# Chunks of 512 tokens, and one TensorE step for the scores of one head pair and the v products of another

## The chip, the cores and the metric

The kernel runs on one core of a Trainium2 chip. The metric is the device time of one execution in microseconds (us). Before the change it was 943.15 us, the median of three runs (941.31 to 943.30).

## The reference

```python
def _attn_ref(q, k, v):                      # [8, 8, 576, 64], fp32
    q_d, k_d, v_d = mean of 4 neighbouring positions of q, k, v      # 144 positions
    out_d = sm_attn(q_d, k_d, v_d)           # softmax(q k^T / 8) v
    out_up = np.repeat(out_d, 4, axis=2)
    mask = np.abs(pos[:, None] - pos[None, :]) < 4                   # a band of 7
    scores = np.where(mask, scale * np.matmul(q, k.transpose(0, 1, 3, 2)), -1e9)
    ... softmax with sum + 1e-9 ...
    return out_up + np.matmul(attn, v)

x = attn_out.transpose(0, 2, 1, 3).reshape(4608, 512)
h = x @ w_in                                 # [4608, 2048]
g = h * np.clip(h + 3.0, 0.0, 6.0) / 6.0
return g @ w_out                             # [4608, 512]
```

(The lines are shortened.) There are two attentions per head, one over pooled positions ("pooled") and one in a band of seven ("banded"); their sum goes through one gated expert layer.

## The kernel before, in words

**The expert layer** is nearly all of TensorE's time. Its tokens go through in chunks (`PART`): 512, 256, then ten of 384. In a chunk there are 16 blocks f of 128 hidden columns. The first product of a block (`gemm1`, L934) is 12 matmuls as wide as the chunk: four pieces of 128 model columns, each as high x high, high x low and low x high, since x and the weights are split into a rounded part and a rest (fp32r). It writes one of two banks, h0 and h1. ScalarE takes relu from it (L940), VectorE the gate (L944), which frees the bank; ScalarE makes the rounded part (L948) and VectorE or GpSimd the rest (L952). The second product (`gemm2`, L986) takes three matmuls of 512 columns for each 128 tokens of the chunk, adds up over the 16 blocks in the o banks (one for each 128 tokens), and follows two blocks behind. ScalarE or VectorE take the o banks out (L882, L884). Each chunk's x is split just ahead of it (`plan_split`, lines 120, 122 and 837), after the last first product of the chunk before.

**The attention** runs in units: one of 8 batches and one of four pairs of heads. Units of batches 0 and 1 ("alone") are worked with TensorE transposes in the start and during the first chunk. From batch 2 on a unit does this: q and k are loaded and turned by VectorE in blocks of 32 (L318), summed over four positions (L327, L331 and L333); TensorE makes the pooled scores (`scores_d4`, L442, 6 matmuls with two records each) and the banded ones (`scores`, L615, 20 matmuls with two records each) in three `a` banks; the pooled softmax is done by ScalarE with sums given out by the exp itself (`weigh`, L463); the banded one adds a mask (L629), takes the greatest (L470), subtracts (L473), one exp over 640 columns (L476), sums (L479), and multiplies by the reciprocal (L492). Both go to memory and come back turned (`put`, `get`, `turn_l`, `turn_d`; L555, L536). Later the v products (`pv`, L656, and `pv_d4`, L570) go into two `a` banks, and the mean (L594, L597) and the additions (L664) write x. The v rows are summed over four by L376 on VectorE or L378 and L379 on GpSimd.

**The order.** A planner (`Plan.emit`) orders all operations before the kernel is built, by a table of costs and due times; each engine then runs its list in that order. Operations name the buffers that they take and free, and the planner gives a slot (`_slots`) when one is free. `plan_duo` makes two units; a unit is a generator, and its second part (v products) is made one unit behind. Scores and v products are operations of their own there.

Of the kernel before, what the change touches and what calls it, by code (L numbers as in the profile page):

```python
# [19 lines left out]
P = 128  # L20
# [36 lines left out]
def tile_local_down_attention_moe(ctx, tc, q_all, k_all, v_all, _qk_loc, _v_loc, w_in, w_out, ident_d, _mask_d, out):  # L57
# [177 lines left out]
    def plan_duo(b, d, masked):  # L235
# [50 lines left out]
        for u in range(2):  # L286
            unit = plan_unit(b, d, u, row0, k0, kv, PS, qk, evicts, users, masked, early_user, due - (1 - u) * unit_time(b))
            next(unit)
            units.append(unit)
            if b < ALONE or len(units) > 1:  # L290
                next(units.pop(0), None)
        if b < BY_PE:
            for kind in "qk":
                plan.free_after(("qkd" + k0, (kind, b, d)), users[kind])

    def plan_unit(b, d, u, row0, k0, kv, PS, duo, evicts, users, masked, early_user, due):
# [11 lines left out]
        def ldt(t, kind):  # L308
            st["raw", kind] = raw = buf("raw" + k0, (kind, un), [P, S // 32, 32])
# [6 lines left out]
        def turn(kind):  # L316
            qk[kind] = buf("qk" + k0, (kind, un), [P, S])
            nc.vector.transpose(out=qk[kind], in_=st["raw", kind].rearrange("p j i -> p (j i)"))  # L318
# [16 lines left out]
        for kind, t in (("q", q_all), ("k", k_all)):  # L335
# [3 lines left out]
            else:  # L339
                rk = "raw" + k0, hk  # L340
                l = op("SP", 2.0, partial(ldt, t, kind), loads if b == 1 else [], take=[rk], size=dma(4 * S, 128), nd=4)
                a = turned[kind] = [op("DVE", 0.66, partial(turn, kind), [l], take=[("qk" + k0, hk)], free=[rk])]
# [88 lines left out]
        def scores_d4():  # L431

            st["psd"] = bank(PS, ("sd", un))
            st["pd"] = buf(pk[0], pk[1], [P, 3, SD])
# [3 lines left out]
            for h, j in ((0, 0), (1, 1), (0, 2), (1, 0), (0, 1), (1, 2)):  # L438
                hs = slice(h * D, (h + 1) * D)
                a, n = QPLACE[h][j]  # L440
                ps = st["ps", 1][:, 5 * D:] if n == 1 else st["psd"][:, n // 2 * SD:]
                nc.tensor.matmul(  # L442
                    ps[a * D:(a + 1) * D, :SD], q4[hs, j * QSTEP:j * QSTEP + QS], k4[hs], start=True, stop=True,
                    skip_group_check=True)
# [4 lines left out]
        def rows_d4(i):  # L449

            if i == 0:
                return [st["psd"][:, :2 * SD].rearrange("p (j k) -> p j k", j=2)] + [st[x][:, ::2] for x in ("pd", "md", "sd")]
            return [st["ps", 1][:, 5 * D:5 * D + SD].unsqueeze(1)] + [st[x][:, 1:2] for x in ("pd", "md", "sd")]
# [23 lines left out]

        def total(x, s):
            nc.vector.tensor_reduce(out=s, in_=x, op=ALU.add, axis=AX.X)  # L479

        def plus(s):
            nc.gpsimd.tensor_scalar(s, s, 1e-9, None, op0=ALU.add)
# [49 lines left out]
        def turn_d(i):  # L532
            if "pdt" not in st:
                st["pdt"] = buf(tk_d[0], tk_d[1], [P, 18 * NAR])
            n, a, e = (P, 0, 12 * NAR) if i == 0 else (NAR, 12 * NAR, 18 * NAR)
            nc.vector.transpose(  # L536
                out=st["pdt"][:n, a:e], in_=st["rd"][:n].rearrange("p j k -> p (j k)")[:, a:e])
# [7 lines left out]
        def get():  # L545
            st["rl"] = raw = buf("rl", un, [P, 20, NAR])
# [6 lines left out]
        def turn_l():  # L553
            st["pt"] = buf("PT" + kv, ("l", un), [P, 5, 2 * D])
            nc.vector.transpose(  # L555
                out=st["pt"].rearrange("p j q -> p (j q)"), in_=st["rl"].rearrange("p j k -> p (j k)"))
# [44 lines left out]
        def scores():  # L601

            st["p"] = buf(pl[0], pl[1], [P, 5, 2, D])
            stats = buf("st" + k0, ("l", un), [P, 2, 12])
            st["m"], st["s"] = stats[:, 0, :NWIN], stats[:, 1, :NWIN]
            for g in range(2 if alone else 0):
# [21 lines left out]
        def outside(g):  # L628
            nc.vector.tensor_tensor(  # L629
# [16 lines left out]
        def pv():  # L646
            if not direct:
# [21 lines left out]
        def tail(eng):  # L669

            if "tail" not in early:
                early["tail"] = xt[0, "tail"] = buf(*xb_of(0), [P, NHP, S - TOK0])
            copy_on(eng, xt[0, "tail"][:, hp], st["px"][1][:, TOK0 - HALF:HALF])
# [6 lines left out]
        def scores_all():  # L680
# [836 lines left out]
```

## Time and profile before

| | us |
|---|---|
| median of three runs | 943.15 |
| lowest, highest run | 941.31, 943.30 |
| span of the profiled execution | 940.1 |
| TensorE busy in it | 925.5 |
| VectorE, ScalarE, GpSimd busy | 564.6, 358.8, 306.1 |

The profile is of one execution; its own time is the span and the little that lies around it, 3.0 us up to the median. In the views that follow, PE is TensorE, PEld its weight loads, DVE VectorE, ACT ScalarE, POOL GpSimd and SP the engine that issues DMAs. A row of grouped instructions gives line, engine, operation, output and input with shapes, the count, then busy us and mean ns of one, then the idle time before them and what ended it. A matmul's busy time overlaps its neighbours', so a product's price is read from the chain, where each row is start, length, engine, output, line and records.

### The profile page before, as it was taken

The numbers are of one execution on the slowest core, as the hardware profiler recorded it, in microseconds if no ns is written. First come the engines' busy times: TensorE is split into PE (matmuls) and PEld (weight loads), VectorE is DVE, ScalarE is ACT, GpSimd is POOL, SyncE is SP. The second block draws the span as 40 slices with busy tenths as digits, with TensorE's granted clock in tenths as the row PEclk, the third lists the DMA queues.
The fourth block names the chain that finished last, engine by engine and source line by source line (L and its number), as shares of the span: only waits on it lengthen the run. The fifth ranks groups of instructions, "written<-read, shape, count | busy, mean of one in ns | idle before, by whom it ended". The sixth has DMA issues, their size and how long they took to land.

```text
span 940.1 us, 19730 instructions
## 1 busy us (share of the span) xinstructions
PE 925.5 (98%) x7525; PEld 803.9 (86%) x7525; DVE 564.6 (60%) x1048; ACT 358.8 (38%) x889; POOL 306.1 (33%) x396
## 2 busy tenths in 40 slices
PE   6999999999999999999999999999999999999997
PEld 4577778989889888889889888988988988998996
DVE  7999987487767566554456667445455654323322
ACT  4799654334333233323333333323233432221322
POOL 4654444244452343332334344225125320000000
PEclk9999999999999999999999999999999999999999
DMA  7997154356666555544235555645154430100101
GB/s 210 311 287 221 30 131 97 67 105 129 125 128 125 108 118 111 101 88 107 39 82 119 101 105 103 129 99 101 37 98 88 104 64 6 35 1 3 32 1 33
DMA packets 311758, 93.52 MB, mean 99 GB/s; under 512 B 251376, under 2 KB 297840, under 8 KB 311664
## 3 DMA queue, kind: packets, MB, share of 16 engines
q1 hardware_dynamic: 311376, 91.83, 43.6%
q8 instruction: 59, 0.97, 0.4%
q10 hardware_dynamic: 288, 0.43, 0.2%
q14 instruction: 35, 0.29, 0.1%
HBM read 69.60 MB, written 22.61 MB: 98 GB/s over the span
## 4 chain that ended last, share of the span: by engine, by line
PE 93%; SPq 2%; DMA 2%; DVE 1%; issue 1%; ACT 1%; POOL 0%; DVEq 0%; ACTq 0%
PE h L934 42%; PE o L986 40%; PE a L656 2%; PE a L615 2%; PE a L442 1%; PE a L570 1%; PE a L986 1%; DMA arena<-in_v_dram 1%; SPq L311 1%; PE o L589 1%; PE a L501 0%; PE a L589 0%; SPq L351 0%; PE a L428 0%; DMA arena<-pl 0%
## 5 line engine op out<-in xcount | busy, mean ns | idle before, releaser
L934 PE MATMUL h<-rounded,wp 128*128 128x384 f32 (+2 forms) x2240 | 418.8, 336 | 0.0
L986 PE MATMUL o<-wp,rounded 128*128 128x512 f32 x1680 | 408.3, 394 | 0.0
L934 PEld LDWEIGHTS h<-rounded,wp 128*128 128x128 f32 x2240 | 383.9, 188 | 14.0 <-issue 1.6
L986 PEld LDWEIGHTS o<-wp,rounded 128*128 128x128 f32 x1680 | 311.0, 188 | 65.8 <-issue 4.2
L940 ACT ACTIVATE arena<-h 128x384 f32<-128x384 f32 (+2 forms) x192 | 93.7, 490 | 366.9 <-PE h L934 365.2
L944 DVE SCALAR_TENSOR_TENSOR arena<-arena,h 128x384 f32<-128x384 f32 (+2 forms) x192 | 104.9, 547 | 183.8 <-ACT arena L940 182.8
L948 ACT CAST rounded<-arena 128x384 fp32r<-128x384 f32 (+2 forms) x192 | 98.2, 512 | 120.5 <-DVE arena L944 120.0
L952 DVE TENSOR_TENSOR rounded<-arena,rounded 128x384 fp32r<-128x384 f32 (+2 forms) x140 | 84.9, 606 | 77.1 <-PE o L986 42.2
L952 POOL TENSOR_TENSOR rounded<-arena,rounded 128x384 fp32r<-128x384 f32 (+2 forms) x52 | 54.5, 1048 | 149.0 <-ACT rounded L948 92.9
L331 POOL TENSOR_TENSOR arena<-arena 128x144 f32<-128x144 f32 x35 | 15.7, 449 | 180.1 <-PE a L442 101.1
L318 DVE STREAM_TRANSPOSE arena<-arena 128x576 f32<-128x576 f32 x56 | 43.2, 772 | 23.7 <-PE a L615 9.0
L333 POOL TENSOR_TENSOR arena<-arena 128x144 f32<-128x144 f32 x70 | 45.1, 644 | 5.5
L492 POOL TENSOR_TENSOR arena<-arena 128x640 f32<-128x640 f32 (+1 forms) x31 | 37.7, 1216 | 18.2 <-DVE arena L485 14.6
L837 POOL TENSOR_TENSOR rounded<-arena,rounded 128x384 fp32r<-128x384 f32 (+2 forms) x12 | 16.3, 1372 | 71.2 <-ACT rounded L120 71.0
L473 POOL TENSOR_TENSOR arena<-arena 128x640 f32<-128x640 f32 x21 | 26.5, 1260 | 27.4 <-DVE arena L470 17.2
L463 ACT ACTIVATE arena<-a,arena 128x144 f32<-128x144 f32 x87 | 32.5, 378 | 1.9 <-DMA arena<-in_v_dram 0.2
L376 DVE TENSOR_REDUCE arena<-arena 128x128 f32<-128x512 f32 (+1 forms) x25 | 26.8, 1072 | 7.2 <-PE a L570 7.1
L536 DVE STREAM_TRANSPOSE arena<-arena 128x384 f32<-128x384 f32 (+1 forms) x48 | 21.4, 461 | 15.2 <-DMA arena<-pd 12.9
L615 PE MATMUL a<-arena 64*64 64x64 f32 x1200 | 30.0, 223 | 0.0
L205 POOL TENSOR_TENSOR wp<-early,wp 128x1024 fp32r<-128x1024 f32 (+1 forms) x9 | 19.3, 2148 | 29.0 <-ACT wp L201 16.8
L615 PEld LDWEIGHTS a<-arena 64*64 64x64 f32 x1200 | 25.6, 134 | 2.1 <-issue 2.1
L656 PEld LDWEIGHTS a<-arena 64*64 64x64 f32 x1120 | 19.1, 134 | 9.3 <-issue 8.1
(194 smaller groups left out, 822.7 us busy)
## 6 DMA issues: line engine op xcount, KB each, us to landing
rawp<-in_w_in_dram SPq DMA_DIRECT2D x16, 512.0 KB
rawp<-in_w_out_dram SPq DMA_DIRECT2D x16, 512.0 KB
arena<-in_q_dram SPq DMA_DIRECT2D x112, 72.0 KB
arena<-in_k_dram SPq DMA_DIRECT2D x112, 72.0 KB
pl<-arena SPq DMA_DIRECT2D x24, 320.0 KB
arena<-pl SPq DMA_DIRECT2D x96, 80.0 KB
arena<-in_v_dram SPq DMA_DIRECT2D x28, 256.0 KB
out_dram<-arena SPq DMA_DIRECT2D x91, 72.0 KB
```

What stands on the lines that cost most here:

```text
L318: nc.vector.transpose(out=qk[kind], in_=st["raw", kind].rearrange("p j i -> p (j i)"))
L333: eng.tensor_tensor(t, t, x[:, :, r], op=ALU.add)
L463: nc.scalar.activation(p[:, j], x[:, j], AF.Exp, bias=m[:, j:j + 1], scale=1.0 / 128.0, accum_out=s[:, j:j + 1])
L492: eng.tensor_tensor(x, x, s.unsqueeze(2).broadcast_to(list(x.shape)), op=ALU.mult)
L615: nc.tensor.matmul(st["ps", g][half:half + WIN, jj * D:jj * D + WIN], qk_of("q")[hs, k_first:k_first + WIN], qk_of("k")[hs, k_first:k_firs ...
L656: nc.tensor.matmul(st["px"][g][h * D:(h + 1) * D, at + lo:at + hi], st["v"][ks, jj, h * D:(h + 1) * D], st["pt"][ks, jj, half + lo:half + ...
L934: nc.tensor.matmul(st["ps"], win[f][:, wt, kk * P:(kk + 1) * P], xs[part][:, kk], start=(kk == 0 and i == 0), stop=(kk == NK - 1 and i == ...
L940: nc.scalar.activation(st["t"], st["ps"], AF.Relu, bias=3.0)
L944: nc.vector.scalar_tensor_tensor(out=t, in0=t, scalar=6.0, in1=st["ps"], op0=ALU.min, op1=ALU.mult)
L948: nc.scalar.copy(st["gh"], st["t"])
L952: eng.tensor_tensor(st["gl"], st["t"], st["gh"].bitcast(F32), op=ALU.subtract)
L986: nc.tensor.matmul(otile[n, m], gt[:, ms], wout[f][:, wt], start=(f == 0 and i == 0), stop=(f == NF - 1 and i == 2),)
```

## The change

- All chunks have 512 tokens (nine). The o banks become four, the `a` banks two. The cost tables of the planner keep their scale (`SHARE`).
- From batch 2 on one operation (`plan_burst`, "a shared step") has the pooled scores of a new unit, both v products of the unit two before it (`DEPTH = 2`), and the banded scores of the new one. It takes both h banks: the v products go there, and the third of the pooled scores that does not fit in the `a` banks, as four matmuls of 72 columns (`rest`), which are copied out (`pull`).
- The turns of q, k and of the weights that come back write over their input (`turn`, `turn_d`, `turn_l`); q, k and the pooled weights share five buffers.
- The banded softmax gets its sums from the exp: ten exps of 64 columns with a bias and a sum (`exps_sums`) take the place of the subtraction, one exp and VectorE's sum. The added 1e-9 goes from GpSimd to ScalarE.
- The buffers between the expert products: three for rounded parts (were four) and two for rests (were three). Due times of the attention (`UNIT_T`, `SLACK`) are others.

```diff
-TOK, TOK0 = 384, 512
+TOK, SHARE = 512, 384
-PART = [(0, TOK0), (TOK0, 2 * TOK - TOK0)] + [(t, TOK) for t in range(2 * TOK, B * S, TOK)]
+PART = [(t, TOK) for t in range(0, B * S, TOK)]
...
+    def plan_burst(unit):
+
+        new = next(unit) if unit else None
+        old = next(units[0]) if len(units) == DEPTH or units and not unit else None
...
+        hx = [(f"h{g}x", key) for g in range(2)]
+
+        def burst():
+            hb = [bank(*h) for h in hx]
+            if new:
+                new["pooled"](hb)
+            if old:
+                old["pv"](hb)
+            if new:
+                new["banded"]()
...
+        o = op("PE", cost, burst, [a for x in both for a in x["after"]], take=hx + [t for x in both for t in x["take"]],
+               free=[t for x in both for t in x["free"]], lag=LAGT, rec=52 * len(both))
...
         def turn(kind):
-            qk[kind] = buf("qk" + k0, (kind, un), [P, S])
-            nc.vector.transpose(out=qk[kind], in_=st["raw", kind].rearrange("p j i -> p (j i)"))
+            nc.vector.transpose(out=qk[kind], in_=qk[kind])
...
+                for i in range(2 if n == 2 else 1):
+                    ks = slice(i * SD // 2, (i + 1) * SD // 2) if n == 2 else slice(0, SD)
+                    ps = rest(h, i) if n == 2 else rows_d4(n)[a * D:(a + 1) * D]
+                    nc.tensor.matmul(
+                        ps, q4[hs, j * QSTEP:j * QSTEP + QS], k4[hs, ks], start=True, stop=True, skip_group_check=True)
+
+        def rest(h, i):
+            return st["hb"][h][i * D:(i + 1) * D, HALF + SD:HALF + SD + SD // 2]
...
+        def exps_sums(first, x, m, s):
+
+            for j in range(first, first + 2):
+                nc.scalar.activation(
+                    x[:, j], x[:, j], AF.Exp, bias=m[:, j:j + 1], scale=0.125, accum_out=s[:, j:j + 1])
...
         def plus(s):
-            nc.gpsimd.tensor_scalar(s, s, 1e-9, None, op0=ALU.add)
+            nc.scalar.activation(s, s, AF.Copy, bias=1e-9)
...
-            ("xb", 2, NHP * S * 4), ("t", 2, TOK * 4), ("rl", 1, NWIN * D * 4), ("ob", 1, 2048), ("raw", 4, S * 4), ("qk", 4, S * 4),
+            ("xb", 2, NHP * S * 4), ("t", 2, TOK * 4), ("ob", 1, 2048), ("raw", 2, 4 * ROW * 4), ("qk", 5, S * 4),
...
-    for key, n in (("gh", 4), ("gl", 3)):
+    for key, n in (("gh", 3), ("gl", 2)):
...
-        ... "a": ["a0", "a1", "a2"], "s": ["a0", "a1", "a2", "o0", "o1", "o2"], "h": ["h0", "h1"],
-        "o0": ["o0"], "o1": ["o1"], "o2": ["o2"], "o3": ["a2"]})
+        ... "a": ["a0", "a1"], "s": ["a0", "a1", "o0", "o1", "o2", "o3"], "h": ["h0", "h1"], "h0x": ["h0"], "h1x": ["h1"],
+        "o0": ["o0"], "o1": ["o1"], "o2": ["o2"], "o3": ["o3"]})
```

What the planner makes of it, at three places. The first is TensorE in the middle of the attention, before: two first products, three second ones, a unit's v products (L656 banded, L570 pooled), and on. (The number behind a name tells buffers apart.)

```order
L934 MATMUL h_4250<-rounded,wp_645 128x384 x12
L986 MATMUL o_3560<-wp_1773,rounded 128x512 x3
L986 MATMUL o_3568<-wp_1773,rounded 128x512 x3
L986 MATMUL o_3575<-wp_1773,rounded 128x512 x3
L656 MATMUL a_4292<-arena 64x60 x2
...
L656 MATMUL a_4293<-arena 64x60 x2
L570 MATMUL a_4292<-arena 64x144 x2
L570 MATMUL a_4293<-arena 64x144 x2
```

And in the changed kernel, with a shared step among 12 second products on either side:

```order
L981 MATMUL h_2362<-rounded,wp_1029 128x512 x12
L1031 MATMUL o_2103<-wp_1149,rounded 128x512 x3
...
L1031 MATMUL o_2163<-wp_1149,rounded 128x512 x3
L472 MATMUL a_2418<-arena 64x144 x2
L472 MATMUL a_2419<-arena 64x144 x2
L472 MATMUL h_2416<-arena 64x72 x2
L472 MATMUL h_2417<-arena 64x72 x2
L709 MATMUL h_2416<-arena 64x60 x2
...
L617 MATMUL h_2417<-arena 64x144 x2
L617 MATMUL h_2416<-arena 64x144 x2
L666 MATMUL a_2418<-arena 64x64 x2
...
L1031 MATMUL o_2103<-wp_1289,rounded 128x512 x3
```

The v products have moved between the two kinds of scores of another unit and from the a banks into the h banks, which the first products before (h_2362) and after it use too.

The second place is VectorE behind v products, before: a v sum (L376), the mean's second half (L597), the additions (L664), then the next rest and gates.

```order
L376 TENSOR_REDUCE arena<-arena 128x128
L597 SCALAR_TENSOR_TENSOR arena<-a_4293,arena 128x144
L485 RECIPROCAL arena<-arena 128x10
L664 TENSOR_TENSOR first<-a_4292,arena 128x288
L664 TENSOR_TENSOR first<-a_4293,arena 128x288
L952 TENSOR_TENSOR rounded<-arena,rounded 128x384
L944 SCALAR_TENSOR_TENSOR arena<-arena,h_4356 128x384
```

In the changed kernel, around a shared step: turns of q and k (L346) stand between the last gates ahead of the step, and a v sum (L403) or a sum of k (L355) beside the mean and the additions (L644, L717).

```order
L346 STREAM_TRANSPOSE arena<-arena 128x576
L991 SCALAR_TENSOR_TENSOR arena<-arena,h_3615 128x512
L346 STREAM_TRANSPOSE arena<-arena 128x576
L991 SCALAR_TENSOR_TENSOR arena<-arena,h_3641 128x512
L999 TENSOR_TENSOR rounded<-arena,rounded 128x512 x2
L403 TENSOR_REDUCE arena<-arena 128x128
L644 SCALAR_TENSOR_TENSOR arena<-h_3690,arena 128x144
L355 TENSOR_REDUCE arena<-arena 128x144
L717 TENSOR_TENSOR arena<-h_3689,arena 128x288
L717 TENSOR_TENSOR arena<-h_3690,arena 128x288
L682 TENSOR_TENSOR arena<-a_3691,mask 128x5x64
```

The gate and the additions have become what frees an h bank for a shared step and for the first product after it.

The third place is TensorE where the first chunk ends, before: 24 second products lie ahead of the next chunk's first product (h_1843).

```order
L986 MATMUL a_941<-wp_1670,rounded 128x512 x3
L986 MATMUL o_874<-wp_1773,rounded 128x512 x3
L986 MATMUL o_882<-wp_1773,rounded 128x512 x3
L986 MATMUL o_888<-wp_1773,rounded 128x512 x3
L986 MATMUL a_941<-wp_1773,rounded 128x512 x3
L934 MATMUL h_1843<-rounded,wp_531 128x256 x12
```

In the changed kernel the scores of batch 2's second unit stand directly ahead of it (h_1972), behind 12 second products:

```order
L1031 MATMUL o_920<-wp_1786,rounded 128x512 x3
L472 MATMUL a_1930<-arena 64x144 x2
L472 MATMUL a_1931<-arena 64x144 x2
L472 MATMUL h_1928<-arena 64x72 x2
L472 MATMUL h_1929<-arena 64x72 x2
L666 MATMUL a_1930<-arena 64x64 x2
...
L981 MATMUL h_1972<-rounded,wp_563 128x512 x12
```

The first scores of batch 2 have moved from the second chunk into the end of the first one.

More of the change, by code (lines that the diff above doesn't have):

```diff
@@ L287, in plan_duo @@
             unit = plan_unit(b, d, u, row0, k0, kv, PS, qk, evicts, users, masked, early_user, due - (1 - u) * unit_time(b))
[L288 to L291, printed above, removed]
+            if b < ALONE:
+                for _ in unit:
+                    pass
+            else:
+                plan_burst(unit)
         if b < BY_PE:
@@ L605, in scores @@
             st["m"], st["s"] = stats[:, 0, :NWIN], stats[:, 1, :NWIN]
+        def scores():
+            if alone:
+                places()
             for g in range(2 if alone else 0):
@@ L646, in pv @@
         def pv():
-            if not direct:
+            if alone and not direct:
                 st["px"] = [bank(PS, ("x", un, g)) for g in range(2)]
@@ L1064, in tile_local_down_attention_moe @@
                 break
-        if not duos and units:
-            next(units.pop(0), None)
+        while not duos and units:
+            plan_burst(None)
         plan_split(n, prev_last)
@@ L1201, in start_of @@
 def start_of(n):
-    return T0 + TC * sum(size for _, size in PART[:n]) / TOK
+    return T0 + TC * sum(size for _, size in PART[:n]) / SHARE
 def need_chunk(b):
```

189 lines of the change are left out of this document (96 added, 93 removed).

## The prediction

> **What bounds the kernel now.** I read the page first (busy times, then the chain that ended last), then the table of stretches, then the list of TensorE's waits, and last the chain row by row.
>
> ```profile
> span 940.1 us, 19730 instructions
> PE 925.5 (98%) x7525; PEld 803.9 (86%) x7525; DVE 564.6 (60%) x1048; ACT 358.8 (38%) x889; POOL 306.1 (33%) x396
> PE 93%; SPq 2%; DMA 2%; DVE 1%; issue 1%; ACT 1%; POOL 0%; DVEq 0%; ACTq 0%
> 60.00:80.00 20.00, 20.00 (x142) 15.36 (x141) 20.00 (x28) 18.45 (x25) 13.41 (x8) 1.00 0.81 239
> 200.00:250.00 50.00, 50.00 (x479) 44.12 (x478) 35.15 (x67) 18.73 (x54) 20.31 (x28) 1.00 0.60 121
> 800.00:900.00 100.00, 100.00 (x510) 91.45 (x509) 31.70 (x54) 25.74 (x51) 1.95 (x1) 1.00 0.06 17
> PE o L638 <- ACT early L120: 0.4, 1, 0.4
> PE a L656 <- ACT arena L463: 0.2, 1, 0.2
> ```
>
> In the stretches the columns are TensorE, its weight loads, VectorE, ScalarE, GpSimd, the granted clock and DMA. TensorE is full in each, at clock 1.00, in the attention stage (200:250) as in the pure matmul stage (800:900). Its waits after the start are fractions of a microsecond. So the time is the start, a sum of TensorE work, and a short end; the other engines count only where they make TensorE wait. Next, TensorE's pieces in the chain (start, length, line, records), from three places:
>
> ```profile
> 130.51 2.72 PE h L934 x12
> 137.86 2.73 PE h L934 x12
> 144.91 2.76 PE h L934 x12
> 177.96 2.87 PE h L934 x24
> 240.86 4.19 PE h L934 x24
> 245.05 0.51 PE a L442 x9
> 245.56 0.06 PE a L615 x2
> 245.62 0.07 PE a L442 x2
> 245.69 0.58 PE a L615 x32
> 246.27 4.35 PE o L986 x18
> 250.62 4.19 PE h L934 x24
> 254.81 0.74 PE a L656 x40
> 255.54 0.48 PE a L570 x12
> 256.03 4.30 PE o L986 x18
> 265.94 4.12 PE o L986 x18
> ```
>
> L934 is the first expert product with 512 (130 to 147), 256 (178) and 384 tokens (241); L986 is the second; L442 and L615 are one head pair's scores, L656 and L570 its v products. One product costs 2.737/12 = 0.2281 us at 512, 2.87/24 = 0.1196 at 256, 4.19/24 = 0.1746 at 384; the second product 4.12/18 = 0.2289.
>
> **The change, part by part.**
>
> *Chunks of 512.* Before: 192 first products at 512, 192 at 256, 10 x 192 at 384: 43.8 + 23.0 + 335.2 = 402.0 us. After: 9 x 192 = 1728 at 512: 394.2. That is -7.8. Ends: with the second product's 0.2289 for all at 512, 402.1 - 395.5, so -6.6; with the cheapest row (2.72/12) 401.7 - 391.7, so -10.0. The second product stays 1728 of the same shape: 0. The gain is the fixed part of 576 products fewer, about 14 ns of each: 174.6 and 228.1 ns lie on a slope of 0.418 ns a column. The Trainium skill ("TensorE: Matmul & The Clock Gate", Back-to-back issue gap) gives N/2.4 + 2.5 ns for one warm product, 576 x 2.5 ns = 1.4 us for this part (an estimate from that page); the rows above show several times its fixed part, and the rows go into the sum.
>
> *One step for two units.* The piece 245.05 to 246.27 is 1.22 us and the next product pays 4.35 - 4.12 = 0.23 more; the v products are 1.22 and 4.30 - 4.12 = 0.18. So each insertion costs about 0.20 to get back to the big products. Also the first block of an insertion is dearer: L442's records take 0.51 + 0.07 = 0.58, L570's 12 of the same width, inside an insertion, 0.48: 0.10. Of 24 units 22 share a step (the first two have scores alone, the last two v products alone): 22 x 0.30 = -6.6. Against it: two of six pooled score products are split into halves of 72, so 8 short records for 4 long ones. L570 gives 0.040 a record at 144, L615 0.58/32 = 0.018 at 64; 8 short ones are about what 4 long ones cost, I take +0.04 a unit, +1.0. Net -5.6. Ends: -6.6, and +3.8 if nothing is saved and each short record costs 0.040 (24 x 0.16).
>
> *The h banks.* The shared step writes its v products and the split scores into h0 and h1, so it waits until both are drained, and the next first product waits until the step's results are.
>
> ```profile
> L940 ACT ACTIVATE arena<-h 128x512 f32<-128x512 f32 x16 | 9.5, 594 | 11.1 <-PE h L934 9.4 <-POOL wp L205 1.6
> L944 DVE SCALAR_TENSOR_TENSOR arena<-arena,h 128x512 f32<-128x512 f32 x16 | 10.7, 675 | 2.5 <-ACT arena L940 2.4
> L594 ACT ACTIVATE arena<-a 128x144 f32<-128x144 f32 x28 | 8.1, 289 | 20.3 <-PE a L570 19.9 <-PE a L586 0.2
> L597 DVE SCALAR_TENSOR_TENSOR arena<-a,arena 128x144 f32<-128x144 f32 x24 | 7.1, 294 | 1.0 <-ACT arena L594 0.8
> L376 DVE TENSOR_REDUCE arena<-arena 128x128 f32<-128x512 f32 x15 | 16.2, 1078 | 6.4 <-PE a L570 6.3
> L664 DVE TENSOR_TENSOR arena<-a,arena 128x288 f32<-128x288 f32 x32 | 13.1, 450 | 0.3
> L318 DVE STREAM_TRANSPOSE arena<-arena 128x576 f32<-128x576 f32 x56 | 43.2, 772 | 23.7 <-PE a L615 9.0 <-POOL arena L331 8.0 <-DMA arena<-in_k_dram 4.8
> L122 DVE CAST rounded<-arena 128x768 fp32r<-128x768 f32 x4 | 2.2, 556 | 0.2 <-PE h L934 0.2
> L120 ACT CAST rounded<-arena 128x768 fp32r<-128x768 f32 x4 | 3.3, 833 | 0.1
> L837 DVE TENSOR_TENSOR rounded<-arena,rounded 128x768 fp32r<-128x768 f32 x3 | 4.1, 1404 | 0.1
> ```
>
> Into the step: the order leaves at least 12 second products (12 x 0.2289 = 2.75 us) between the last first product and a shared step; relu and gate need 0.594 + 0.675 = 1.27, about 1.5 with hand-overs: 1.2 spare. Out of it: 0.64 of banded scores, 0.2 of return and 2.75 of second products = 3.6, against mean 0.289, its second half 0.294, a v sum of 1.078 that stands between them in VectorE's order, one addition 0.450: 2.1, about 2.4 with hand-overs: again 1.2 spare. 15 of the 26 steps have only 12 products on one side; elsewhere 24 double the cover. So 0 there, covered by second products. One place lacks cover: at the end of the first chunk the second scores step is followed at once by the first product of the next chunk. From the last first product, ScalarE has the cast of 896 columns (833 x 896/768 = 0.97), two exps (0.30 each, below), relu 0.59; then gate 0.68, two small low parts (about 0.25 each) and one of 896 (1.404 x 896/768 = 1.64) on VectorE: about 5.2 us, where TensorE has 2.75 + 1.25 = 4.0. I take +1.2, ends 0 and +2.4.
>
> *Banded exp sums on ScalarE; in-place turns; other buffers.* Ten exps with sums replace one exp, and GpSimd's subtraction and VectorE's sum go.
>
> ```profile
> 17.11 0.38 ACT L463 ACTIVATE arena<-a,arena 128x144 f32<-128x144 f32 x1
> 17.48 0.37 ACT L463 ACTIVATE arena<-a,arena 128x144 f32<-128x144 f32 x1
> L476 ACT ACTIVATE arena<-arena 128x640 f32<-128x640 f32 x29 | 21.2, 730 | 3.0 <-POOL arena L473 2.3 <-DVE arena L473 0.5
> L473 POOL TENSOR_TENSOR arena<-arena 128x640 f32<-128x640 f32 x21 | 26.5, 1260 | 27.4 <-DVE arena L470 17.2 <-issue 6.0 <-PE h L934 4.3
> L479 DVE TENSOR_REDUCE arena<-arena 128x10 f32<-128x640 f32 x28 | 22.6, 806 | 1.5 <-ACT arena L476 1.4
> ```
>
> Start to start 0.37 at 144 columns, near 0.30 at 64 (relu: 594 ns at 512): 3.0 us a unit for 0.73, some +2.3; with four bank copies and small ones about +3.5 x 24 = 84 us on a ScalarE busy for 359 of 940. GpSimd loses 1.26 and VectorE 0.81 a unit. None is on the chain, and a unit's softmax gets hardly longer: 3.0 us of exps for 0.73 + 1.26 + 0.81 = 2.8. Its cover grows: the v products come two steps later, and the closest shared steps are 60 big products apart, 16 us with the step. If that did not do, VectorE would stand at the next unit's masking, and the gates behind it. The turns keep their count and shape; q and k of the unit two ahead, and the weights read back, now share five buffers, each for one interval. Their DMAs and SP's number of issues are the same: 0. The first 42 us and the last product's way out stay: 0, and I allow 1 us either way.
>
> **Sum.** -7.8 - 5.6 + 1.2 = -12.2: a profiled span near 928. The profiled execution's 940.1 lies 3.0 under the median of the runs, 943.15; the same 3.0 stay, so 943.15 - 12.2 = 931.0.
>
> **Rivals.**
>
> 1. *Slower: the h banks drain late.* The mechanism is VectorE's order: gate or addition stands behind work that was not started in time. One turn and one v sum ahead (0.77 + 1.08) eat the 1.2 and 0.65 more: 15 x 0.65 = 9.8, 940.8. With a second turn 1.42: +21.3, 952.3. It decides at 12.2/15 = 0.8 a step. For it: turns wait for DMA (4.8 us in their row), a step needs both banks and two units' inputs, one late input stops both. Against: the stretches show VectorE at 35 of 50 in the attention stage, and TensorE waits almost nowhere. Not faster: 0.20, of which 0.04 within the bound.
>
> 2. *The shared step saves nothing* (the return cost follows the number of small blocks, or short records cost as long ones): -7.8 + 0 to 3.8 + 1.2, 936.6 to 940.4. For it: the saving is read from differences of 0.1 to 0.2. Against: L570 costs 0.48 behind L656 with no break. 0.12.
>
> 3. *The fixed part isn't per product*, so that larger chunks gain nothing: 943.15 - 5.6 + 1.2 = 938.8. The three widths above speak against it. 0.04. The 2.5 ns of the Trainium skill ("TensorE: Matmul & The Clock Gate", Back-to-back issue gap) would be this case with 1.4 us of gain, 937.4; the trace does not bear it out.
>
> 4. *Instruction supply.* A shared step has 112 products and 112 weight loads in 2.4 us.
>
> ```profile
> q8 instruction: 59, 0.97, 0.4%
> 21.54:24.21 2.67, 2.67 (x88) 1.77 (x87) 2.02 (x5) 2.20 (x13) 1.67 (x4) 1.00 0.72 175
> ```
>
> 0.97 MB in 59 packets is 16 KB each; the start ran 88 products and 87 loads in 2.67 us without a break, the nearest row and below the step's rate. If half of the 22 steps lost 1.2 us, +13: 944. The Trainium skill ("Runtime: NRT & Kernel Launch", Instruction fetch mechanics) says that 16 KB blocks are fetched while the current one runs, mostly hidden; no row shows a stall. 0.02.
>
> **How the numbers follow.** Forecast 0.62 (its own range 924 to 936), rival 1 0.20, rival 2 0.12, rival 3 0.04, rival 4 0.02. The low end: -10.0 - 6.6 + 0 gives 926.6, with 1 us at the start and the spread of the runs (2 us) 924. The high end takes rivals 2 and 3 and the near half of rival 1: 943. A measurement here tells 0.2%, 1.9 us, from nothing. Faster 0.78, same 0.04, slower 0.18.
>
> **What would show it.** Right: TensorE full from 47 us on; first products 2.74 per 12; one 2.3 to 2.5 us insertion where two of 1.22 stood; at most small waits for VectorE. Wrong: TensorE waits of 0.5 us and more, many times, whose releaser is the addition, the gate or the bank copies, or a DMA into the step's v products; an insertion near 2.9; first products over 0.229 us each.

## The result, and the profile after

The changed kernel takes 926.14 us (median of four runs, 924.45 to 927.57) against 942.68 us (941.31 to 943.30) for the kernel before beside it: a ratio of 0.9823 with a 95% interval of 0.9806 to 0.9840. In a second comparison it was 927.38 against 942.93, 0.9831 (0.9811 to 0.9852). The forecast was 931.0 with its own range of 924 to 936: the direction and the mechanisms held, the gain of 12.2 us was taken 3.4 to 4.4 us too small (16.5 and 15.6 in the two comparisons).

The page of the changed kernel, its span and busy times:

```profile
span 925.0 us, 19239 instructions
PE 907.6 (98%) x7045; PEld 734.4 (79%) x7045; DVE 552.5 (60%) x979; ACT 440.2 (48%) x1443; POOL 233.8 (25%) x310
```

Two of its stretches, in the attention stage and in the pure product stage (TensorE, weight loads, VectorE, ScalarE, GpSimd, granted clock, DMA share, GB/s):

```profile
200.00:250.00 50.00, 49.59 (x511) 40.92 (x510) 32.18 (x63) 27.09 (x116) 15.94 (x25) 1.00 0.65 133
800.00:900.00 100.00, 100.00 (x442) 82.78 (x442) 31.15 (x44) 23.54 (x38) 0.00 (x0) 1.00 0.04 11
```

And its list of TensorE's waits behind 49 us (us in total, times, longest):

```profile
PE h L981 <- DVE arena L991: 1.3, 1, 1.3
PE h L981 <- DVE arena L717: 0.6, 1, 0.6
PE h L981 <- DVE first L717: 0.6, 2, 0.4
PE o L1031 <- POOL rounded L999: 0.4, 1, 0.4
PE h L981 <- ACT arena L120: 0.3, 1, 0.3
```

TensorE is still the bound, full at clock 1.00 but for 0.4 us in the stretch from 200 on. New are small waits of the first product (L981) for its h bank, in which the gate (L991), the additions (L717) and the copies (L120) are named; none lies behind 400 us. ScalarE is at 440.2 us, where 443 was forecast. The prices of TensorE's pieces, from the chain (start, length, line, records):

```profile
190.05 0.41 PE a L472 x8
190.46 0.13 PE h L472 x8
190.59 0.58 PE h L709 x40
191.16 0.36 PE h L617 x10
191.52 0.04 PE a L666
191.56 0.09 PE h L617 x2
191.65 0.58 PE a L666 x28
192.23 5.67 PE o L1031 x24
197.90 5.44 PE h L981 x24
203.34 2.72 PE o L1031 x12
277.14 5.44 PE o L1031 x24
```

A shared step (pooled scores L472, v products L709 and L617, banded scores L666) takes 2.18 us, and the products behind it 5.67 - 5.44 = 0.23 more. Both kinds of product cost 5.44/24 = 0.2267 us. The profiled executions (940.1 and 925.0, 15.1 apart) are compared below in two ways. The middle column takes these rows for every product and step. The last one sums all TensorE records behind the start, from each one's start to the next one's with the waits taken out; its third row holds all small blocks, with what the big products beside them pay over their price.

| | forecast | by the rows after | summed over the records |
|---|---|---|---|
| first products: 402.0 before, 1728 x 0.2267 = 391.7 | -7.8 | -10.3 | -8.5 |
| second products: 0.2289 before, 0.2267 | 0 | -3.8 | -2.5 |
| 22 shared steps: 2 x (1.22 + 0.20) before, 2.18 + 0.23 | -5.6 | -9.5 | -9.8 |
| waits of TensorE from 49 us on: 0.18 before, 3.15 | +1.2 | +3.0 | +3.0 |
| end of the start (46.36 and 49.08 us, rows with the second execution below) | 0 | +2.7 | +2.7 |
| sum | -12.2 | -17.9 | -15.1 |

The rows overshoot the 15.1 measured by 2.8, the sum over the records meets it. The difference lies in the big products. The rows 4.19/24 and 4.12/18 of the kernel before hold a change of width between neighbours (below), which not every run of products pays, and a few runs of the changed kernel cost more than 0.2267 a product (1.1 us over it in all).

How one of the waits arises, in the chain (SPq is the issue on SyncE's queue):

```profile
243.39 0.50 SPq L340
243.93 2.38 DMA arena<-in_k_dram
246.34 0.78 DVE arena L346
248.45 0.46 DVE first L717
249.04 3.02 PE h L981 x12
```

A load of k is issued late, its turn (L346) stands in VectorE's list ahead of the additions (L717), these free the h bank, and the first product of 249.04 comes 0.41 us late. That is rival 1's mechanism, at 249, 266 and 363 us (0.41, 0.63, 0.17) and not at 15 places.

### The profile page after: what moved, and what is told of

Same layout as the page of the kernel before. It is cut to its first block, busy times and chain, and to the rows that moved or that the text cites. A ratio compares the mean times of both kernels' runs of the same rounds, so it can differ in the third digit from the quotient of the medians.

```text
span 925.0 us, 19239 instructions
## 1 busy us (share of the span) xinstructions
PE 907.6 (98%) x7045; PEld 734.4 (79%) x7045; DVE 552.5 (60%) x979; ACT 440.2 (48%) x1443; POOL 233.8 (25%) x310
## 4 chain that ended last, share of the span: by engine, by line
PE 87%; DMA 3%; DVE 3%; ACT 3%; SPq 2%; issue 1%; POOL 1%; ACTq 0%; DVEq 0%; POOLq 0%
PE h L981 40%; PE o L1031 39%; PE a L666 2%; PE h L709 1%; DMA arena<-in_v_dram 1%; PE h L617 1%; ACT arena L522 1%; PE a L472 1%; PE o L636 1%; SPq L340 1%; DMA arena<-in_k_dram 1%; DMA out_dram<-arena 1%; DMA early<-in_v_dram 0%; ACT arena L987 0%; POOL rounded L999 0%
## 5 line engine op out<-in xcount | busy, mean ns | idle before, releaser
L981 PE MATMUL h<-rounded,wp 128*128 128x512 f32 x1728 | 405.6, 390 | 2.8 <-DVE arena L991 1.3
L981 PEld LDWEIGHTS h<-rounded,wp 128*128 128x128 f32 x1728 | 322.9, 188 | 72.0 <-DVE arena L991 1.6
L987 ACT ACTIVATE arena<-h 128x512 f32<-128x512 f32 x144 | 85.7, 595 | 195.5 <-PE h L981 183.6
L991 DVE SCALAR_TENSOR_TENSOR arena<-arena,h 128x512 f32<-128x512 f32 x144 | 98.0, 681 | 126.1 <-ACT arena L987 125.8
L999 DVE TENSOR_TENSOR rounded<-arena,rounded 128x512 fp32r<-128x512 f32 x110 | 81.5, 741 | 125.3 <-PE o L1031 105.9
L995 ACT CAST rounded<-arena 128x512 fp32r<-128x512 f32 x144 | 89.0, 618 | 114.6 <-PE o L1031 63.9
L522 ACT ACTIVATE arena<-arena 128x64 f32<-128x64 f32 x240 | 80.3, 337 | 0.2
L999 POOL TENSOR_TENSOR rounded<-arena,rounded 128x512 fp32r<-128x512 f32 x34 | 46.3, 1363 | 77.5 <-ACT rounded L995 40.8
L346 DVE STREAM_TRANSPOSE arena<-arena 128x576 f32<-128x576 f32 x56 | 42.6, 764 | 23.0 <-DMA arena<-in_k_dram 18.2
L405 POOL TENSOR_TENSOR arena<-arena 32x256 f32<-32x256 f32 (+1 forms) x29 | 22.3, 768 | 114.1 <-DMA arena<-in_v_dram 81.2
L522 ACT ACTIVATION_READ_ACCUMULATOR arena<-arena 128x1 f32 x240 | 45.3, 189 | 0.0
L361 POOL TENSOR_TENSOR arena<-arena 128x144 f32<-128x144 f32 x58 | 36.5, 630 | 4.5
L403 DVE TENSOR_REDUCE arena<-arena 128x128 f32<-128x512 f32 (+1 forms) x23 | 24.4, 1060 | 11.7 <-PE h L617 10.9
L603 DVE STREAM_TRANSPOSE arena<-arena 128x640 f32<-128x640 f32 x24 | 20.2, 844 | 16.8 <-DMA arena<-pl 16.7
L666 PE MATMUL a<-arena 64*64 64x64 f32 x1160 | 29.1, 224 | 0.0
```

Source lines behind the costliest of these rows:

```text
L346: nc.vector.transpose(out=qk[kind], in_=qk[kind])
L361: eng.tensor_tensor(t, t, x[:, :, r], op=ALU.add)
L403: eng.tensor_reduce(out=vd, in_=raw.rearrange("p r e -> p e r"), op=ALU.add, axis=AX.X)
L522: nc.scalar.activation(x[:, j], x[:, j], AF.Exp, bias=m[:, j:j + 1], scale=0.125, accum_out=s[:, j:j + 1])
L666: nc.tensor.matmul(st["ps", g][half:half + WIN, jj * D:jj * D + WIN], qk_of("q")[hs, k_first:k_first + WIN], qk_of("k")[hs, k_first:k_firs ...
L981: nc.tensor.matmul(st["ps"], win[f][:, wt, kk * P:(kk + 1) * P], xs[part][:, kk], start=(kk == 0 and i == 0), stop=(kk == NK - 1 and i == ...
```

## The experiments

Each was timed beside the kernel before; ratios are to that kernel.

### Chunks of 384 again

```diff
-TOK, SHARE = 512, 384
+TOK, SHARE = 384, 384
```

> The changed kernel with twelve chunks of 384 tokens; the shared step and all else stay. My theory: a first product of 384 columns costs 0.1746 us with its share of the change of width, and every run of second products pays 0.04 us more when the first products beside it are of another width (4.12 us for 18, 2.76 for 12, 7.52 for 33 before, each 0.2267 a product and 0.04; 5.44 for 24 in the changed kernel). So first products 402 for 392 and second ones about +3.8: +14 us, 926 becomes 940. Rival A: the second products became cheaper by the shared step, not by the chunks: they stay at 0.2267, +10 us, 936. Rival B: the fixed part is not per product: within 2 us of 926.

970.99 us, ratio 1.0295 (1.0278 to 1.0313): 45 us more than the changed kernel, far beyond either expectation. The prices came out as my theory had them, in its chain:

```profile
324.17 4.12 PE o L1031 x18
328.29 4.18 PE h L981 x24
```

Its list of TensorE's waits, the two largest behind the start:

```profile
PE o L1031 <- DVE arena L931: 5.3, 1, 5.3
PE h L981 <- DVE arena L991: 4.7, 5, 1.5
```

And a stretch of it, with the granted clock at 0.93:

```profile
150.00:200.00 50.00, 44.69 (x260) 39.14 (x259) 20.18 (x39) 17.80 (x66) 7.39 (x10) 0.93 0.22 47
```

The second product is back at 4.12/18 = 0.2289 with the shared step kept, so the chunks set that price and rival A falls. The rest is waits: 21.3 us of them behind 49 us, where the changed kernel has 3.15, and the granted clock falls behind the long ones (0.93 over 150 to 200). Behind the longest wait it is 0.50 from 167 to 173 us. I read it so that the steps and the waits for banks that fit between groups of 24 second products did not fit between groups of 18; no run shows that by itself. Of the 43.6 us between the spans the waits are 18.2 and the 14 of the theory are in line with the prices; how the rest divides between the clock, the start and the steps is left open.

### The fixed part of a product by itself

```diff
+                    for c in (slice(0, DM // 2), slice(DM // 2, DM)):
                         nc.tensor.matmul(
-                            otile[n, m], gt[:, ms], wout[f][:, wt],
+                            otile[n, m][:, c], gt[:, ms], wout[f][:, wt, c],
...
```

> The changed kernel with every second product cut into two of 256 columns: the same columns in twice the products, 1728 more. This measures the fixed part of a product by itself. By the rows of before and after, (2.87 - 0.04)/24 = 0.1179 us at 256 and 0.2267 at 512: 9 ns for each added product, +15.8 us, and up to 0.08 us more for each of some 80 runs of second products, since their neighbours are now of another width: 942 to 948. By the 2.5 ns of the Trainium skill (TensorE: Matmul & The Clock Gate, Back-to-back issue gap) 1728 x 2.5 ns = 4.3 us: 930. If the fixed part is not per product: 926.

(In this kernel the sums of one half of the columns lack their first product.) 948.65 us, ratio 1.0069 (1.0051 to 1.0087): 22.5 us more than the changed kernel. The chain in the pure product stage:

```profile
812.68 5.47 PE h L981 x24
818.15 5.75 PE o L1032 x48
```

5.75/48 = 0.1198 us at 256 columns. Two of them are 0.2396 for 0.2267: 12.9 ns for each added product, 22.3 us over 1728, nearly the whole difference. It was expected at 9 ns, because 0.04 us for a change of width had been taken off the row at 256; the run of 256 columns pays none (from its third product on each takes 0.120 us), so the fixed part is the larger one. The first products pay 0.03 for their neighbours' other width (5.47 for 5.44). The 2.5 ns of the Trainium skill (TensorE: Matmul & The Clock Gate, Back-to-back issue gap) does not hold for these products.

### The shared steps taken apart, v products in the a banks

```diff
-        o = op("PE", cost, burst, ...)
+        hx = [("a" if part == "v" else f"h{g}x", (x["un"], part, g)) for g in range(2)]
+            return op("PE", 1.35, run, x["after"], take=hx + x["take"], ...), hx
...
+            units.pop(0).send(one(old, "v"))
+            unit.send(one(new, "s"))
```

> The changed kernel with its shared steps taken apart: a head pair's v products are a step of their own, in the two a banks, two units behind its scores; the scores keep their step, with the split third in the h banks. My theory, read from the trace of the changed kernel: a shared step is 2.18 us and 0.23 to get back, two steps were 1.22 and 0.20 each, so 0.43 a pair: 22 pairs, +9.5 us, 935.6, less 0.4 for each pair that falls side by side, plus waits. Rival A, the prediction's sizes: 0.30 a pair less the split scores' 1.0: +5.6, 931.7. Rival B, a shared step saves nothing: 926 within 2. In the trace the v step should be 1.22 again under theory and near 1.0 if its records had become cheaper by the banks they write.

950.95 us, ratio 1.0088 (1.0069 to 1.0108): 25 us more, where 9.5 and waits were expected. Its chain, with a scores step and a v step:

```profile
320.22 0.41 PE a L469 x8
320.63 0.12 PE h L469 x8
320.75 0.58 PE a L663 x40
321.34 2.95 PE o L1028 x12
324.28 2.72 PE h L978 x12
327.00 0.74 PE a L706 x40
327.74 0.48 PE a L614 x12
328.23 2.99 PE h L978 x12
```

Its largest wait, and two stretches at one of the places:

```profile
PE a L469 <- ACT arena L526: 9.1, 4, 2.3
```
```profile
364.00:366.00 2.00, 0.04 (x2) 0.07 (x3) 2.00 (x5) 2.00 (x12) 1.34 (x4) 1.00 0.52 130
368.00:370.00 2.00, 2.00 (x6) 1.59 (x5) 0.96 (x3) 1.84 (x10) 1.34 (x1) 0.50 0.77 231
```

A scores step is 1.11 and 0.23, a v step 1.22 and 0.27: 2.83 for the shared step's 2.41, or 0.42 a pair, 9.2 us. Of that 0.15 is blocks (1.11 + 1.22 for 2.18: the v products start at 0.74 for 40 records alone and at 0.58 behind the pooled scores, so that the block that stands first pays) and 0.27 the second return. The scores were 1.22 before and are 1.11 with the split: the short records are 0.11 cheaper, not dearer. Rivals A and B fall by these rows. The spans are 26.2 us apart. Beside the 9.2 there are 9.6 us of waits (12.7 for 3.15 behind 49 us), five of 2.3 us where a scores step follows a v step at once, and the clock: at 0.50 behind each, so that the 48 products from 367.40 on took 12.69 us for 10.88, five times 1.8. That is 27.8 in all, 1.6 over the difference of the spans. (L526 in the line of waits is the added 1e-9 of a softmax. At the same time, from 365.40 us on, VectorE does the additions that read the a banks, behind the mean and a turn of 0.77 us; one of the five waits is put down to them. The mean on ScalarE, which the next expectation names, had ended at 364.03.)

### The same with the v products in the h banks

The edit is shown against the kernel of the last run.

```diff
-            hx = [("a" if part == "v" else f"h{g}x", (x["un"], part, g)) for g in range(2)]
+            hx = [(f"h{g}x", (x["un"], part)) for g in range(2)]
```

> Once more the shared steps taken apart, now with the v products in the h banks, as in the shared step. In the run with a banks the rows gave 1.22 + 0.27 and 1.11 + 0.23 us for a pair against 2.18 + 0.23, 0.42 a pair or 9.2 us in all, but five scores steps waited 2.3 us for ScalarE's mean, and the clock fell to 0.50 behind each. My theory: without those waits +9.2 us on 926, some 935, and each wait in it of over 2 us costs as much again by the clock. Rival: taking the h banks twice makes the first products wait, 0.3 to 0.6 us at each of 22 steps: 942 to 948.

957.9 us, ratio 1.0186 (1.0164 to 1.0207); blocks and returns as in the last run (1.22 + 0.27, 1.11 + 0.23). TensorE waits 22.3 us behind 49 us:

```profile
PE h L706 <- ACT arena L120: 8.0, 2, 7.8
PE h L978 <- DVE arena L988: 6.7, 4, 2.0
```

The rival was right in kind, in fewer and longer waits than it said, and the time lies beyond its 942 to 948: 1.0 to 2.6 us at seven places behind 200 us and 7.8 at one, where two scores steps stand in a row ahead of a v step. My theory of 935 has been measured in neither form: both orders without shared steps wait. So the 9 us for the blocks stand on rows of the chain, and what the shared step spares in waits depends on the order.

### The banded softmax as before

```diff
-            a = op("ACT", 0.2, lambda: nc.scalar.activation(st["m"], st["m"], AF.Copy, scale=-0.125), [a])
...
-                a = op("ACT", 0.62, lambda j=j: exps_sums(j, p_all(), st["m"], st["s"]), [m, a])
...
+            subs = [op(on("minus", 10 * D), 0, lambda eng: minus(eng, p_all(), p_all(), st["m"]), [a], lock=True)]
...
+        a = op("ACT", 0.2 + size / 1150, lambda: exps(p_all(), 0.125), subs)
+        a = op("DVE", 0.15 + size / 960, lambda: total(p_all(), st["s"]), [a])
+        a = op("POOL", 0.35, lambda: plus(st["s"]), [a])
...
```

> The changed kernel with the banded softmax as before: a subtraction on VectorE or GpSimd, one exp of 640 columns, the sum on VectorE, the 1e-9 on GpSimd. Prediction's step: the exps are off the path, 0 within 1 us. Rival A: the ten exps make the weights late, the issue of the weights' way to memory holds back the loads of k behind it on SyncE's queue, and the turn of that k stands ahead of the additions on VectorE; then the waits of 0.3 to 0.6 us at 162, 249, 266 and 363 us go: -1.5 us. Rival B: VectorE with 0.8 us more a unit makes the h banks late: +2 to +5 us.

924.5 us, ratio 0.9818 (0.9787 to 0.9850): not to be told from the changed kernel's 0.9823. VectorE is busy 580.1 us for 552.5, ScalarE 379.3 for 440.2, and TensorE waits 2.7 us behind 49 us for 3.15. The waits at 166, 255 and 264 us (0.69, 0.71, 1.00) are no smaller than those they replace, so rival A falls too. The prediction's 0 stands: this part of the change moves work between engines that do not bound it.

### The added 1e-9 back on GpSimd

```diff
-            nc.scalar.activation(s, s, AF.Copy, bias=1e-9)
+            nc.gpsimd.tensor_scalar(s, s, 1e-9, None, op0=ALU.add)
...
```

> The changed kernel with nothing but the added 1e-9 of both softmaxes back on GpSimd. The stretch of 21 first products that ends the start begins at 46.36 us before, 49.08 in the changed kernel, and 47.76 with the banded softmax as before, which has this too. Theory: the short instruction in ScalarE's list costs the start about 1.3 us: the stretch begins near 47.8, and the time is 1.3 us less, 924.8. Rival: the start moves by the order of its loads and not by this: 49.1 within 0.5.

924.93 us, ratio 0.9820 (0.9803 to 0.9838): the time of the theory, but not separable from the changed kernel. The stretch of 21 products begins at 46.25, earlier than either side said; since that start varies by execution (below), it says little on either. What goes with this part is elsewhere: the 1.3 us for the gate (L991) ahead of the next first product. It stands in every kernel of this study with chunks of 512 that has the 1e-9 on ScalarE, and in none of those with it on GpSimd; the order of the first chunk differs by it. In exchange this kernel waits 1.65 us at 246.

### Filling products in the start

```diff
-                busy(o.busy)
+                busy(3 * o.busy if 7 < o.start < 15 else o.busy)
+            if o.start < 19 and getattr(getattr(o.fn, "func", None), "__name__", "") == "sum_pe":
+                sums += 1
+                if sums == 3:
+                    busy(7)
```

> The changed kernel with more filling products on TensorE in the start: nine in place of three ahead of the turn of rows that waited 2.15 us at 12 us, and seven ahead of the sum of v that waited 1.58 us at 22.9 us. My theory: TensorE's clock was granted at 0.50 from 12 to 16 us and from 23 to 26.4 us because TensorE had stood still; with filling it stays at 1.00, and the second stretch, 3.5 us of products at 0.51, takes half: -1.5 us, 924.6. Rival: loads and the softmaxes on VectorE set the start, and the clock is hidden behind them: 0 within 0.5. Either way the granted clock of 22.9 to 26.4 us tells whether standing still was the cause.

931.37 us, ratio 0.9872 (0.9850 to 0.9894): slower than the changed kernel. The stretch at 24 us of the changed kernel:

```profile
24.00:26.00 2.00, 2.00 (x44) 1.21 (x42) 0.56 (x1) 1.37 (x8) 1.42 (x3) 0.50 0.95 263
```

The same of this kernel, and its new wait:

```profile
24.00:26.00 2.00, 1.45 (x11) 0.80 (x11) 2.00 (x6) 0.83 (x2) 0.98 (x2) 1.00 0.87 320
```
```profile
PE a L691 <- ACT first L120: 2.6, 1, 2.6
```

Standing still was the cause of the 0.50: filled, the clock stays at 1.00, and the transposes (L691) that began at 40.01 us begin at 36.81. But then TensorE waits 2.6 us for a copy that ScalarE holds back until a piece of the weights (a transfer of 5.7 us) has landed, and behind this wait the clock falls all the same:

```profile
42.00:44.00 2.00, 2.00 (x7) 1.07 (x7) 1.85 (x5) 1.91 (x5) 0.97 (x1) 0.50 0.96 357
```

The start hangs on loads, as the rival said, but the time is far from its 0; my theory fell. Of the 5 us that this kernel is slower, its profiled span (926.6) shows 1.6. That profile is of its fastest run (928.44), beside the changed kernel's slowest (927.57); the others have no profile, and what they lost is not explained.

### The changed kernel itself again

No edit; the kernel of the result, timed once more.

> The changed kernel itself, beside the two that follow. Its profiled execution began the stretch of 21 first products at 49.08 us; kernels with the same order up to there began it at 47.75 and 46.82. My theory: the start of one execution varies by its loads; it begins anywhere from 46.5 to 50, the first shared steps come at the same times as before within 0.5 us all the same, and the time is 926 within 1.5. Rival: the start of the changed kernel is late in each execution: 49.1 within 0.3.

927.38 us, ratio 0.9831 (0.9811 to 0.9852), span 923.5. The stretch of 21 first products in its chain:

```profile
46.71 5.00 PE h L981 x21
```

In the chain of the first profiled execution, and of the kernel before:

```profile
49.08 5.00 PE h L981 x21
```
```profile
46.36 4.99 PE h L934 x21
```

The start does vary by execution, so that the +2.7 of the table belongs to one execution and not to the change. That the first steps come at the same times was wrong: the second scores step is at 157.1 for 160.1. The gain is partly lost again: this execution waits 4.6 us behind 49 us (1.69 of it at 248) for 3.15.

### An order with later landings

```diff
-                    end = dma_free + 0.8
+                    end = dma_free + (0.8 if t < 150 else 2.5)
```

> The changed kernel with the banded softmax as before (924.5 us alone) and an order made as if every transfer after the start landed 1.7 us later, so that the turns and v sums that wait for one stand later in VectorE's list. Theory: the waits for VectorE at 166, 255 and 264 us (0.69, 0.71, 1.00) come from turns and v sums that wait for transfers with gates and additions behind them; they go, -1.5 to -2.4 us, 922 to 923. Rival: SyncE issues without a break there and VectorE is full; the waits move and stay: within 1 us of 924.5.

With the softmax of the kernel before, 923.82 us, ratio 0.9803 (0.9789 to 0.9817), span 920.5; waits behind 49 us 1.4 for 2.7. The waits fell as the theory said, but the time did not come to its 922 to 923: 0.7 us below the 924.5 is within the rival's 1 us. It is the fastest kernel of the study, but the intervals of 0.9803, 0.9818 and 0.9823 overlap: that it beats the changed kernel is not shown.

### Both together

The exps stay on ScalarE.

```diff
-            nc.scalar.activation(s, s, AF.Copy, bias=1e-9)
+            nc.gpsimd.tensor_scalar(s, s, 1e-9, None, op0=ALU.add)
...
-                    end = dma_free + 0.8
+                    end = dma_free + (0.8 if t < 150 else 2.5)
```

> The changed kernel with the added 1e-9 on GpSimd and an order made as if transfers landed 1.7 us later; the exps stay on ScalarE. Theory: the wait of 1.3 us at 55 to 57 us goes with the first (plus_pool had 0.32 in its place), the waits for VectorE at 246 to 363 us with the second (late_loads had 1.4 us of waits after the start, the changed kernel 3.15): 926.1 - 1.2 - 1.5 = 923.4. Rival: what goes at one place comes back at another, as in plus_pool, which waited 1.65 us at 246: 925 to 926.

929.31 us, ratio 0.9861 (0.9831 to 0.9891): the rival, and worse than it. The waits go to new places (2.2 us in three waits for the o banks' way out, 1.4 for the additions at 299). Its profiled execution, one of the slower ones (931.9), began the stretch of 21 products at 52.4; with two waits of 0.70 and 0.88 us near 39 us the clock fell to 0.50 for 10 us, in which TensorE was busy:

```profile
42.00:46.00 4.00, 4.00 (x16) 1.45 (x16) 1.71 (x4) 3.91 (x5) 1.29 (x1) 0.50 1.03 410
```

From that stretch to the end it took 877.7 us, the changed kernel 875.9 from 49.08 on. So the gains of 1 us at one place did not add up, with the start left out either.

### The v products of the last unit instead of the second last

```diff
-DEPTH = 2
+DEPTH = 1
```

> The changed kernel with the v products of the last unit in a step in place of the second last one's. The prediction took it that two steps of delay cover the weights' way through the softmax and memory. Theory: with one step of delay the way, some 8 us of softmax and 8 us of transfers, does not fit where steps lie 14 us apart, and the step waits for its turned weights: 1 to 3 us at every fourth step, twice that with the clock, +5 to +20 us, 931 to 946. Rival: TensorE's order spreads the steps and the delay costs nothing: 926 within 1.

1074.7 us, ratio 1.1394 (1.1374 to 1.1414). Its largest wait, in the list of TensorE's waits:

```profile
PE h L709 <- DVE arena L603: 93.8, 6, 18.6
```

One of the six in the order of time (start, length, engine, line, then idle before and who ended it), for a unit whose scores were made at 259.08; and the stretch ahead of it:

```profile
282.97 1.40 PE L709 MATMUL h<-arena 64*64 64x60 f32 x39 [15.02 <-DVE arena L603]
```
```profile
268.00:282.00 14.00, 0.00 (x0) 0.00 (x0) 2.84 (x6) 2.01 (x13) 0.00 (x0) 0.50 0.59 125
```

From a unit's scores to its turned weights (L603) 23.9 us pass. Five times the order puts two steps three products apart, and the v products stand in the middle of a step, so the whole TensorE waits 15 us, with the clock at 0.50 behind it. The sixth wait is for the last unit, whose v products stand 12 products behind its scores. The other steps, 27 us and more behind the scores that they need, do not wait for L603. The theory had the mechanism, at far too small a size. In the changed kernel two steps of delay are 32.7 us at the tightest (227.4 to 260.1), which covers the 23.9, and its closest steps are 16 us apart, which would not. Whether an order with its steps further apart would do with one step of delay was not tried.

## Why the prediction was right, point by point

- **The bound.** Right: TensorE is full at clock 1.00 to the end, and the time followed the sum of its work. Of the 4.9 us between forecast and result 2.9 lie in the spans (15.1 for 12.2). That this is so little is partly luck: TensorE's work fell by 20.8 where 13.4 was forecast, and waits and the start took 5.7 back where 1.2 was forecast. The other 1.9 is the choice of execution: the four runs take 1.9 to 3.0 us more than their spans, and the profiled one (927.57, span 925.0) is the slowest of them, so that the median lies only 1.1 us over its span where 3.0 had been carried over.
- **First products.** Right in mechanism, and nearly in size: -7.8 forecast, -8.5 summed over the records. The price was a little high: it took 0.2281 from three pieces (2.72, 2.73, 2.76) of the first chunk, which is interrupted all the time; uninterrupted products cost 0.2267, the cheapest row, which stood as the end -10.0.
- **Second products.** The term 0 was wrong. It took "the same shape" for the same price; 4.12 for 18 holds 0.04 us for a change of width between neighbours (4.12 = 18 x 0.2267 + 0.04; 7.52 = 33 x 0.2267 + 0.04). In the records of before it lies in the first nine products of a run (229, 234, 235, 224, 231, 236, 229, 232 and 231 ns from start to start at 827 us, 226 or 227 behind them). With all products 512 wide it is gone: -2.5 summed, -3.8 if every run had paid it. The runs with chunks of 384 and with halves showed it from both sides.
- **Shared step.** Right in mechanism, mis-sized: -5.6 forecast and -9.5 by the rows (-9.8 summed), beyond its end of -6.6. This is the largest miss of the sum. Three sizes: the first block's share is 0.15 and not 0.10; the return saved is 0.17 and not 0.20; and the split scores, taken at +0.04 a unit, are 0.10 cheaper. A short record costs 0.12/8 = 0.015, less than half a long one (0.48/12 = 0.04).
- **h banks.** +1.2 forecast, all of it at the end of the first chunk; there 0.28 was lost, and 0.41, 0.63 and 0.17 at three steps that were taken at 0. In sum 1.5 (2.4 in the second execution). The cover of 12 second products was enough at nearly all tight steps.
- **Exps, turns, buffers.** 0 in the time, as forecast, and shown for the exps by their run. The turns and the buffers were not run by themselves; of TensorE's waits only one of 0.4 us, for a rest (L999), can be theirs. Not foreseen was the 1.3 us wait in the first chunk that goes with the 1e-9 on ScalarE.
- **Start.** 0 forecast within 1; +2.7 in one execution and +0.3 in the other.
- **Rivals.** Late h banks behind steps occurred at three or four places instead of 15. "Saves nothing" and "not per product" are refuted by the rows of the steps taken apart and of the halves. Instruction supply: of the 22 shared steps 21 took 2.17 to 2.18 us and one 2.30, so nothing stalled there.

## What to carry to other kernels

Price an operation from a run of it whose neighbours are as they will be after the change: a row of 18 products here carried a cost that belonged to the neighbours' width. Joining small blocks between large products saves the first block's share and the return, 0.4 us a pair here, but only with a delay that covers the way of its inputs (23.9 us) and banks that drain in time; the same blocks taken apart cost 25 to 32 us, most of it waits and the clock behind them. On a full TensorE a wait of some 2 us can cost nearly twice its length, since the clock may fall behind it (2.3 us of wait and 1.8 of clock in the steps taken apart).

## What the runs showed of the hardware that was not expected

- The fixed part of one of these products (fp32r, a weight load for each) is 12.9 ns: 0.1198 us at 256 columns and 0.2267 at 512 lie on the slope of 0.418 ns a column that the prediction's rows gave.
- A change of width costs a run of 512 wide products behind narrower ones 0.03 to 0.04 us, and a run of 384 wide ones behind 512 wide ones 0.02; a run of 256 wide ones pays nothing (start to start, as above).
- The granted clock fell to 0.50 behind waits of 1.6 to 2.6 us (1.58 us at 22.9 in the changed kernel's start, 2.3 us five times in the first run of the steps taken apart, 2.6 us in the filled start), and stayed there some 3.4 us (23.0 to 26.4 us in the changed kernel's start). The length of a wait does not decide it alone: in the run of both together two waits of 0.70 and 0.88 us were enough, and it stayed for 10 us, while 1.69 us at 248 us of the second execution and 2.04 us in the second run of the steps taken apart left it at 1.00, here the latter:

```profile
620.00:622.00 2.00, 0.28 (x2) 0.00 (x0) 1.09 (x2) 1.25 (x5) 0.00 (x0) 1.00 0.92 146
622.00:624.00 2.00, 1.69 (x7) 1.42 (x8) 1.92 (x5) 1.24 (x3) 1.01 (x1) 1.00 0.55 118
```

What else decides it is open. The Trainium skill (TensorE: Matmul & The Clock Gate, What's actually happening) has the clock fall after an idle window of about 3.4 us; here shorter waits did it, and the 3.4 us of work until it is released agree in most places, though not in the run of both together.
